# One row of score, state and y matmuls per chunk, keys transposed from the rotated rows, and an engine order set by a list of moves

## The chip, the cores and the metric

The kernel runs on one core of a Trainium2 chip. A core has five engines that run side by side, each with its own in-order instruction stream: TensorE (PE) multiplies matrices and writes to PSUM, a small memory of eight banks of 2 KB per partition; VectorE (DVE), ScalarE (ACT) and GpSimd (POOL) work on tensors elementwise; SyncE (SP) only issues transfers (DMAs). Engines wait for each other through semaphores. The metric is device time of one execution in microseconds. The kernel before took 684.2 us (median of three runs, 683.13 to 686.0).

## The reference

A gated linear recurrence (GateLoop) on 4 x 8 heads, 768 steps, head size 48, is followed by a SwiGLU feed-forward on 3072 tokens (384 to 1536 to 384). All is fp32. What is computed:

```python
mag = np.sqrt(a_re * a_re + a_im * a_im)
scale = np.minimum(mag, 0.999) / (mag + 1e-06)
a_re_n, a_im_n = (a_re * scale, a_im * scale)
for t in range(S):
    new_re = ar * S_re - ai * S_im
    new_im = ar * S_im + ai * S_re
    kv = np.einsum('bhd,bhe->bhde', k[:, :, t], v[:, :, t])
    S_re, S_im = (new_re + kv, new_im)
    y[:, :, t] = np.einsum('bhd,bhde->bhe', q[:, :, t], S_re)
...
rms = np.sqrt(np.mean(x * x, axis=-1, keepdims=True) + 1e-06)
xn = x / rms * rms_g
g = xn @ w_gate
silu = g * (1.0 / (1.0 + np.exp(-g)))
val = xn @ w_val
return (silu * val @ w_out).astype(np.float32)
```

## The kernel before

**Chunks.** The 768 steps of each of the 4 sequences are cut into 6 chunks of 128, which gives 24 chunks (n = 0 to 23). Within a chunk the recurrence is a masked attention; between chunks a state per head is carried on. The gates are turned into sizes and angles beforehand, and keys and queries are scaled and rotated by them (`gates`, lines 1138 to 1234). The rotation leaves six row blocks of 128 partitions x 256 columns per chunk (three times the cosine, three times the sine part; columns 0 to 127 are keys, 128 to 255 queries), in `rot` and, from chunk 4 on, also in `kin`. Six DMAs on SP (line 1229) put these rows into `kq`, 96 partitions x 8 heads x 256. Units of two chunks share the gate work; chunks 0 and 1 are units of their own.

**One chunk on TensorE** (`attend`, lines 1247 to 1355):

- *Scores* S, in two halves a = 0, 1 of four heads each: 16 fp32 matmuls of 32 output rows each (line 1262), then one COPY_PREDICATED on DVE per half ("the mask") that takes the causal part into `am`. For chunks 0 to 3 the halves use banks 4 and 5; from chunk 4 (`LATER`) on both use bank 5, so the second half waits for the first half's mask.
- *y* into bank 6: 16 matmuls on `am` and `ve` and, unless the sequence starts, 16 on the old state and the queries.
- *Transposes*: eight of 96 x 128 keys out of `kq`, copied by ACT to `kt`; *state* T: 24 matmuls of `kt` and `vn` into bank 5, then two DVE operations that make the new state. The last chunk of a sequence (n = 5, 11, 17, 23) has neither.
- *norm*: square of y, its sum over features by a matmul with ones (bank 7), then `ssv` on ACT, then a power of -1/2 on POOL (line 1335), a broadcast of that number, and a product on DVE that writes `xT`, the input of the feed-forward, out of bank 6.

Scores, y and state are written in column tiles of 32 (the profile shows them as 96*32 and 128*32); all other matmuls use the array whole (128*128 or 96*128).

**Feed-forward.** Pairs of chunks make 12 groups. Groups 0 and 1 use plain products; from group 2 on gate and value products follow a fast scheme with 15 products on sums of blocks (`joint`, `STEPS`, `PRODUCTS`), and the output product uses seven block products (`down`).

**Order.** Nothing is issued as it is written. `fast` fills a list of operations with estimated durations and dependencies (`Flow.add`, line 579); a whole PSUM bank counts as one place. `Flow.schedule` (line 617) plays that list through: at each step the engine that is free first takes its ready operation with the earliest due time. Due times follow from the last user backwards, plus a table of shifts by stage (`flow.shift`). The result is a fixed order for each engine. In the first 62 us of the plan, `Flow.warm` puts idle matmuls ("fillers", on `rot`, bank 3) where the plan has TensorE wait (lines 707 to 713). Their number comes from the planned gap: one for each 0.43 us at first, one for each 0.26 us later.

**Weights** arrive as pairs of 32-bit words and are converted by ACT and DVE (`narrow`); POOL issues these transfers in the order of pieces.

Of the kernel before, what the change touches and what calls it, by code (L numbers as in the profile page):

```python
# [14 lines left out]
ALU = mybir.AluOpType  # L15
# [485 lines left out]
class Flow:  # L501
# [15 lines left out]
    def __init__(self, nc, rooms):  # L517
        self.nc = nc
        self.rooms = rooms
        self.ops = []  # L520
        self.seen = {}
        self.stage = None
        self.shift = {}
        self.warm = None
        self.fillers = []

# [52 lines left out]
    def add(self, eng, calls, dur, reads=(), writes=(), table=None, land=None, due=None, after=(), behind=(), late=None, mode=None, group=None):  # L579
        over = self.OVERLAP.get(eng, 0.0) if land is None else 0.0  # L580
        shy = eng == "POOL" and land is None and calls[0][0] == self.nc.gpsimd.tensor_tensor
# [12 lines left out]

    def dates(self):
        users = [[] for _ in self.ops]
        self.next = [[] for _ in self.ops]
        for op in self.ops:
# [18 lines left out]
    def schedule(self):  # L617
        users = self.dates()
        left = [len(op["deps"]) + len(op["behind"]) for op in self.ops]
# [4 lines left out]
        mode = last = None  # L624
# [21 lines left out]
        while True:  # L646
            best = None
            for eng, ops in waiting.items():
                if ops:
# [29 lines left out]
            for o in waiting[eng]:  # L679
                if ready[o["i"]] > t + 1e-9:  # L680
# [9 lines left out]
            if eng in self.patient:  # L690
# [13 lines left out]
            if eng == "PE":  # L704
                dur += self.between(o, last)
                mode, last = o["mode"], o
            if eng == "PE" and self.warm and not claimed and t < self.warm["until"] and all("end" in x for x in self.warm["after"]):
                since = max([free["PE"]] + [x["end"] + 0.06 for x in self.warm["after"]])
                step = 0.26 if recent else 0.43
                n = int((t - since - 0.25) / step)  # L710
                if n > 0:
                    self.fillers.append((order - 0.5, n))
                    recent.append((since, since + step * n))
# [35 lines left out]
def fast(tc, ctx, qT, kT, v, a_re, a_im, w_gate, w_val, w_out, rms_g, out, H, bad):  # L749
# [171 lines left out]
    room("pad0", [P, 3])  # L921
# [47 lines left out]
    for t in banks[4:6]:  # L969
# [42 lines left out]
    def fetch(i, piece, raw, eng):  # L1012
# [12 lines left out]
        pace = dict(load=1.9 + 1.0e-3 * raw.shape[1], lead=1.2) if eng == "POOL" else dict(slow=2.5)  # L1025
# [48 lines left out]
    SUMMED = ()  # L1074
    LIGHT = (0, 1, 2)
    SENT = range(4, N - 2)
    turn = {}
    moved = {}
    HOLD = 1
# [58 lines left out]
    def gates(u):  # L1138
# [72 lines left out]
        for i, n_ in enumerate(ns):  # L1211
# [11 lines left out]
            rows[n_] = [o[:, j] for o in turned for j in range(ND)]  # L1223
        for i, n_ in enumerate(ns):
# [4 lines left out]
            moved[n_] = [dma(kq[r:D2:2 * ND], x, "SP", slow=0.3) for r, x in enumerate(rows[n_])]  # L1229
# [17 lines left out]
    def attend(n):  # L1247
# [12 lines left out]
        k, q = kq[:, :, 0:C], kq[:, :, C:2 * C]  # L1260
        for a in range(2):
# [11 lines left out]
            o = am[:, a * HH:(a + 1) * HH]  # L1273
            add("DVE", [(nc.vector.copy_predicated, (), dict(out=pairs(o), mask=mask, data=pairs(s)))],
                0.2 + 1.04e-3 * HH * C, [causal, s, o], [o])
        flow.stage = "y", n
# [476 lines left out]
```

## Time and profile before

| | |
|---|---|
| median of three runs | 684.2 us (683.13 to 686.0) |
| the profiled execution | 682.97 us |
| its span, first to last instruction | 681.2 us |
| busy: TensorE, VectorE, ScalarE, GpSimd | 646.5, 556.8, 499.4, 66.8 us |
| mean granted TensorE clock | 0.999 |

The page of the profile gives totals, the waits name who waited for whom, the windows give busy time by stretch, and the timeline lists instructions in order of time. A timeline row has the start, the time from first start to last end, the engine, the line, the operation with out<-in, the stationary and moving shapes, and xN, the number of records; fp32 products have two records each, transposes one. A square bracket gives idle time of that engine before the row and who ended it. Nearly all instructions carry line 746, since one loop issues them all, so groups are told apart by names: `bank<-kq` is S, `bank<-am,ve` and `bank<-kq,state` together are y, `bank<-vn,kt` is T, `bank<-ident,kq` the transposes. A row's second number overlaps the next row; for the cost on TensorE the distance from start to start counts.

### The profile page before, as it was taken

The numbers are of one execution on the slowest core, as the hardware profiler recorded it, in microseconds if no ns is written. First come the engines' busy times: TensorE is split into PE (matmuls) and PEld (weight loads), VectorE is DVE, ScalarE is ACT, GpSimd is POOL, SyncE is SP. The second block draws the span as 40 slices with busy tenths as digits, with TensorE's granted clock in tenths as the row PEclk, the third lists the DMA queues.
The fourth block names the chain that finished last, engine by engine and source line by source line (L and its number), as shares of the span: only waits on it lengthen the run. The fifth ranks groups of instructions, "written<-read, shape, count | busy, mean of one in ns | idle before, by whom it ended". The sixth has DMA issues, their size and how long they took to land.

```text
span 681.2 us, 19019 instructions
## 1 busy us (share of the span) xinstructions
PE 646.5 (95%) x7914; PEld 603.4 (89%) x7917; DVE 556.8 (82%) x1026; ACT 499.4 (73%) x864; POOL 66.8 (10%) x109
## 2 busy tenths in 40 slices
PE   0689999999999999999999999999999999999997
PEld 0678877886899999999999999998999999999997
DVE  8989999989998969879989869789879787246463
ACT  8649657995685774775778777777669686699872
POOL 3121034011000100011010100101000000000000
PEclk9999999999999999999999999999999999999999
DMA  9798483454425521354543522455250437725410
GB/s 280 264 240 238 125 239 98 113 125 94 106 51 99 140 36 52 95 114 86 142 84 60 134 68 50 109 122 141 40 111 17 105 115 149 254 95 189 160 47 27
DMA packets 104155, 81.98 MB, mean 120 GB/s; under 512 B 41952, under 2 KB 94560, under 8 KB 104064
## 3 DMA queue, kind: packets, MB, share of 16 engines
q1 hardware_dynamic: 98560, 64.68, 35.5%
q0 software_dynamic: 4416, 15.35, 10.9%
q8 instruction: 63, 1.03, 0.6%
q10 hardware_dynamic: 1088, 0.69, 0.3%
q14 instruction: 28, 0.23, 0.1%
HBM read 55.84 MB, written 4.72 MB: 89 GB/s over the span
## 4 chain that ended last, share of the span: by engine, by line
issue 33%; PE 32%; DVE 13%; DMA 9%; ACT 7%; POOL 2%; SPq 2%; POOLq 0%; DVEq 0%; ACTq 0%
PE bank L746 32%; DMA sq<-rs 4%; SPq L746 2%; ACT L746 2%; DMA wo<-in_w_gate_dram 2%; DVE hT L746 2%; DVE turns L746 2%; ACT t L746 1%; DVE wo L746 1%; POOL rs L746 1%; DVE rot L746 1%; DVE t L746 1%; ACT in L746 1%; DVE wv L746 1%; DVE wg L746 1%
## 5 line engine op out<-in xcount | busy, mean ns | idle before, releaser
L746 PE MATMUL bank<-wo,hT 128*128 128x192 f32 (+1 forms) x696 | 140.8, 350 | 0.0
L746 PEld LDWEIGHTS bank<-wo,hT 128*128 128x128 f32 x696 | 115.0, 190 | 11.6 <-DVE hT L746 0.5
L746 PE MATMUL bank<-xT,wg 128*128 128x128 f32 (+1 forms) x488 | 84.3, 305 | 1.6 <-ACT sg L746 1.6
L746 PE MATMUL bank<-xT,wv 128*128 128x128 f32 (+1 forms) x488 | 82.6, 301 | 0.0
L746 ACT ACT_TABLE_LOAD x57 | 73.1, 1283 | 9.7 <-DVE rot L746 4.8
L746 PEld LDWEIGHTS bank<-xT,wg 128*128 128x128 f32 x488 | 70.6, 191 | 6.8 <-ACT sg L746 1.8
L746 ACT ACTIVATE hT<-bank 128x512 f32<-128x512 f32 x100 | 58.1, 594 | 21.5 <-PE bank L746 19.2
L746 PEld LDWEIGHTS bank<-xT,wv 128*128 128x128 f32 x488 | 70.0, 192 | 3.2 <-issue 0.2
L746 POOL TENSOR_TENSOR rs<-ssv,mhalf 128x1 f32<-128x1 f32 x24 | 21.0, 877 | 442.0 <-ACT ssv L746 388.7
L746 DVE TENSOR_TENSOR hT<-hT 128x768 f32<-128x768 f32 (+1 forms) x60 | 51.7, 863 | 0.4
L746 PE MATMUL bank<-yg,wg 128*128 128x128 f32 x320 | 50.7, 281 | 0.0
L746 PE MATMUL bank<-yg,wv 128*128 128x128 f32 x320 | 48.8, 275 | 0.0
L746 ACT ACTIVATE bank<-bank 128x512 f32<-128x512 f32 x60 | 35.1, 586 | 18.2 <-PE bank L746 11.6
L746 DVE TENSOR_TENSOR hT<-bank,hT 128x512 f32<-128x512 f32 x50 | 34.4, 688 | 13.5 <-ACT bank L746 5.4
L746 DVE COPY_PREDICATED am<-causal,bank 128x512 f32<-128x512 int32 x48 | 34.8, 734 | 12.7 <-PE bank L746 12.5
L746 ACT ACTIVATE sg<-bank 128x256 f32<-128x256 f32 (+1 forms) x72 | 38.4, 534 | 8.7 <-DVE bank L746 4.7
L746 PE MATMUL bank<-sums,hT 128*128 128x192 f32 x240 | 44.7, 329 | 0.0
L746 PEld LDWEIGHTS bank<-yg,wg 128*128 128x128 f32 x320 | 42.2, 191 | 1.3 <-issue 0.2
L746 PEld LDWEIGHTS bank<-yg,wv 128*128 128x128 f32 x320 | 42.2, 192 | 0.0
L746 PEld LDWEIGHTS bank<-sums,hT 128*128 128x128 f32 x240 | 39.1, 190 | 0.3
L746 ACT ACTIVATE turns<-in 128x768 f32<-128x768 f32 (+1 forms) x39 | 30.6, 792 | 11.2 <-DVE in L746 5.8
L746 PEld LDWEIGHTS bank<-kq 96*32 96x32 f32 x1536 | 30.4, 110 | 9.4 <-issue 3.6
(217 smaller groups left out, 1451.4 us busy)
## 6 DMA issues: line engine op xcount, KB each, us to landing
kq<-rot SPq DMA_DIRECT2D x84, 128.0 KB, 2.4
kq<-kin SPq DMA_DIRECT2D x60, 128.0 KB, 2.6
kin<-in_q_dram SPq DMA_DIRECT2D x24, 192.0 KB, 3.0
kin<-in_k_dram SPq DMA_DIRECT2D x24, 192.0 KB, 3.7
in<-in_a_re_dram SPq DMA_DIRECT2D x11, 384.0 KB, 4.2
in<-in_a_im_dram SPq DMA_DIRECT2D x11, 384.0 KB, 4.5
out_dram<-ot SPq DMA_DIRECT2D x22, 192.0 KB, 2.2
vn<-in_v_dram SPq DMA_DIRECT2D x20, 192.0 KB, 2.9
```

What stands on the lines that cost most here:

```text
L746: fn(*args, **kw)
```

## The change

1. *Row.* S of both halves, T and y (in two parts) of one chunk are bound into a chain from chunk 4 on: the planner, once it has placed one link, places the next link as TensorE's next operation. T goes ahead of y.
2. *Banks.* From chunk 4 on the halves of the scores use banks 5 and 6 (6 is also y's), state uses bank 7, the transposes banks 7 and 5. Bank 6 is cleared once at the start, as 4 and 5 were.
3. *Transposes* read the six rotated row blocks (128 x 128 each) in place of `kq`, three in each half; ACT puts the columns in order as it copies.
4. *Two roots.* For chunks 0 and 1 the power on POOL becomes a reciprocal root and a square on ACT and two operations on DVE.
5. *Planner.* Fillers are counted in another way, modelled durations of some transfers change, the table of shifts is another, masks and transposes have stages of their own, and after a first pass a list of some 1,200 moves (`flow.moves`: put operation o behind operation x) rearranges the order of all five engines; a second pass only computes times for that order, with fillers counted anew. In the second pass a chain need not stay unbroken: its links keep their order, and a move can put another operation between two of them.

```diff
@@ class Flow
+    def chain(self, ops):
+        for o in ops[1:]:
+            ops[0]["deps"] |= {d for d in o["deps"] if d < ops[0]["i"]}
+        for o, x in zip(ops, ops[1:]):
+            o["then"] = x["i"]
+            x["deps"].add(o["i"])
...
     def schedule(self):
+        self.run()
+        if self.moves:
...
+            for eng, moves in self.moves.items():
+                out = {o for o, _ in moves}
+                line = [o for o in lines[eng] if o not in out]
+                for o, behind in moves:
+                    line.insert(line.index(behind) + 1 if behind >= 0 else 0, o)
+                lines[eng] = line
+            self.fillers = []
+            self.run(lines)
...
+                if eng == "PE" and bound is not None and not lines:
+                    ops = [o for o in ops if o["i"] == bound]
...
-                step = 0.26 if recent else 0.43
-                n = int((t - since - 0.25) / step)
+                left_ = t - since - 0.25
+                hot = sum(e - max(b, since - 4.0) for b, e in recent if e > since - 4.0)
+                n = int(left_ / 0.24 if hot >= 2.0 else left_ / 0.43 if left_ < 3.9 else 9 + (left_ - 3.9) / 0.24)
@@ fast
-    for t in banks[4:6]:
+    for t in banks[4:7]:
         fill(t, 0.0, eng="DVE", due=-300.0)
...
-        pace = dict(load=1.9 + 1.0e-3 * raw.shape[1], lead=1.2) if eng == "POOL" else dict(slow=2.5)
+        pace = dict(load=1.9 + (0.8e-3 if i < 4 else 1.0e-3) * raw.shape[1], lead=1.2) if eng == "POOL" else dict(slow=2.5)
...
+            k_rows[n_] = [x[:, 0:C] for x in rows[n_]]
...
-            moved[n_] = [dma(kq[r:D2:2 * ND], x, "SP", slow=0.3) for r, x in enumerate(rows[n_])]
+            moved[n_] = [dma(kq[r:D2:2 * ND], x, "SP", slow=0.3 if n_ < 2 else 0.8) for r, x in enumerate(rows[n_])]
@@ attend
+        if not last:
+            kt = kts[0]
+            flow.stage = "kt", n
+            for a in range(2):
+                ps = banks[7 - 3 * a] if n < LATER else banks[7 - 2 * a]
+                kp = ps[:, 0:ND * P].rearrange("t (j x) -> t j x", j=ND)
+                ks = k_rows[n][a * ND:(a + 1) * ND]
+                calls = [(nc.tensor.transpose, (kp[:, j], ks[j], ident), {}) for j in range(ND)]
+                add("PE", calls, ND * 0.115, [*ks, ident], [kp])
+                o = kt.rearrange("t h (l a j) -> t a h l j", a=2, j=ND)[:, a]
+                act(o, kp.rearrange("t j (l h) -> t h l j", h=H), AF.Copy)
+        chain = []
         for a in range(2):
-            ps = banks[4 + a] if n < LATER else banks[5]
+            ps = banks[4 + a] if n < LATER else banks[5 + a]
...
-            mms(list_, HH // 2 * 0.285, due=EARLY.get(n), mode=BLK)
+            chain.append(mms(list_, HH // 2 * 0.285, due=EARLY.get(n), mode=BLK))
...
+        if not last:
+            ps = banks[5 if n < LATER else 7][0:D2, 0:DM]
+            chain.append(mms([(st[c * BLK:(c + 1) * BLK, h], kt[:, h, c * BLK:(c + 1) * BLK], vv[:, h], True, True)
+                 for h in range(H) for c in range(3)], H * 0.1, mode=BLK))
...
-        order = [lines[c][i] for i in range(len(lines[0])) for c in range(4)]
-        mms(order, len(order) * mm_time(C) / 4, mode=BLK)
+        early = 1 if first else 2
+        for part in (range(early), range(early, len(lines[0]))):
+            chain.append(mms([lines[c][i] for i in part for c in range(4)], len(part) * mm_time(C), mode=BLK))
+        if n >= LATER:
+            flow.chain(chain)
...
+        if n in NEWTON:
+            x, y = rss[n % 2], news[n % 2]
+            act(x, sv, AF.Abs_reciprocal_sqrt)
+            act(y, x, AF.Square)
+            stt(y, y, -0.5, sv, ALU.mult)
+            stt(x, y, 1.5, x, ALU.add)
+        else:
+            add("POOL", [(nc.gpsimd.tensor_tensor, (), dict(out=rss[n % 2], in0=sv, in1=mhalf,
+                                                            op=ALU.pow))], 0.56, [sv, mhalf], [rss[n % 2]])
...
+    flow.moves = {
+        "POOL": (
+            (9, 0), (2, 9), (11, 12), (15, 11), (4, 13), (17, 148), (5, 17), (10, 5), (14, 143),
...
```

More of the change, by code (lines that the diff above doesn't have):

```diff
@@ L525, in __init__ @@
         self.fillers = []
+        self.moves = {}
     def delay(self, o, x):
@@ L597, in dates @@
         self.next = [[] for _ in self.ops]
+        for op in self.ops:
+            op.pop("landed", None)
+            op.pop("end", None)
         for op in self.ops:
@@ L617, in schedule, with run @@
     def schedule(self):
+        self.run()
+        if self.moves:
+            lines = {}
+            for o in sorted(self.ops, key=lambda o: o["order"]):
+                lines.setdefault(o["eng"], []).append(o["i"])
+            for eng, moves in self.moves.items():
[6 more added lines that the diff above has]
+            self.run(lines)
+    def run(self, lines=None):
         users = self.dates()
+        turn = dict.fromkeys(lines or (), 0)
         left = [len(op["deps"]) + len(op["behind"]) for op in self.ops]
@@ L623, in schedule @@
         table = None
-        mode = last = None
+        mode = last = bound = None
         for op in self.ops:
@@ L679, in schedule @@
             for o in waiting[eng]:
-                if ready[o["i"]] > t + 1e-9:
+                if ready[o["i"]] > t + 1e-9 or eng == "PE" and bound is not None and not lines and o["i"] != bound or lines and o["i"] != lines[eng][turn[eng]]:
                     continue
@@ L689, in schedule @@
             o = pick[1]
-            if eng in self.patient:
+            if lines:
+                turn[eng] += 1
+            elif eng in self.patient:
                 for x in waiting[eng]:
@@ L920, in fast @@
     most = room("most", [P, 1])
-    room("pad0", [P, 3])
+    news = [room(f"new{i}", [P, 1]) for i in range(2)]
+    room("pad0", [P, 1])
     W = 4 * P
@@ new lines, in fast @@
+        ("look", 10): -15.7, ("look", 12): -0.1, ("look", 17): -50.1, ("mask", 3): -62.9, ("mask", 6): -3.4,
+        ("mask", 11): -48.4, ("mask", 16): -30.8, ("mask", 22): -57.2, ("mask", 23): -53.7, ("norm", 7): 0.3,
+        ("norm", 8): -3.5, ("norm", 9): -1.0, ("norm", 10): -13.9, ("norm", 17): 11.2, ("norm", 20): -4.5,
+        ("norm", 22): 0.1, ("norm", 23): -33.7, ("raw", 0): -8.9, ("root", 7): -5.6, ("root", 10): 71.9,
+        ("root", 11): 44.5, ("root", 12): 25.9, ("rot", 0): -3.5, ("rot", 5): 19.5, ("rot", 6): 75.5,
@@ new lines, in fast @@
+        ("rot", 7): 25.0, ("rot", 9): 5.0, ("rot", 10): 22.7, ("rot", 11): 0.1, ("rot", 12): -1.8,
+        ("scale", 0): -8.7, ("size", 0): -2.3, ("size", 2): -1.9, ("size", 3): 1.2, ("size", 4): -67.2,
+        ("size", 5): 22.7, ("size", 6): 16.1, ("size", 8): 40.2, ("size", 9): 0.3, ("size", 10): 28.1,
+        ("size", 11): 49.7, ("size", 12): 5.9, ("state", 2): 39.4, ("turn", 0): 2.2, ("turn", 1): -9.0,
+        ("turn", 3): 36.6, ("turn", 4): -5.8, ("turn", 7): -0.2, ("turn", 9): 52.9, ("turn", 10): -2.5,
@@ new lines, in fast @@
+        ("turn", 11): 1.8, ("turn", 12): 0.1, ("w", 1): 75.8, ("w", 2): -0.6, ("w", 3): -4.1, ("w", 6): 27.7,
+        ("w", 9): -3.1, ("w", 10): 66.5, ("y", 0): 6.0, ("y", 2): -1.5, ("y", 6): 0.2,
+    }
+    flow.moves = {
+        "POOL": (
+            (9, 0), (2, 9), (11, 12), (15, 11), (4, 13), (17, 148), (5, 17), (10, 5), (14, 143),
+            (6, 126), (7, 6), (149, 154), (179, 184), (197, 2326),
+        ),
+        "ACT": (
[42 rows of a table added]
+        ),
+        "DVE": (
[66 rows of a table added]
+        ),
[33 rows of a table added]
+        ),
[32 rows of a table added]
+        ),
```

79 lines of the change are left out of this document (32 added, 47 removed), and 173 rows, old and new, of the table filler.

## The prediction, made before the changed kernel was run

> **What bounds the kernel now.** I read the page first, then TensorE's waits, then two windows.
>
> ```profile
> span 681.2 us, 19019 instructions
> ...
> PE 646.5 (95%) x7914; PEld 603.4 (89%) x7917; DVE 556.8 (82%) x1026; ACT 499.4 (73%) x864; POOL 66.8 (10%) x109
> ```
> ```profile
> PE bank L746 <- DVE ot L746: 16.9, 1, 16.9
> PE bank L746 <- DVE rot L746: 6.4, 1, 6.4
> PE bank L746 <- ACT sg L746: 1.6, 1, 1.6
> ```
> ```profile
> 0.00:52.00 52.00, 26.31 (x450) 24.52 (x451) 45.03 (x76) 34.27 (x60) 14.10 (x37) 1.00 0.88 263
> 120.00:620.00 500.00, 497.42 (x6360) 468.48 (x6365) 416.16 (x792) 375.26 (x647) 35.35 (x55) 1.00 0.43 100
> ```
>
> The first window column after the length is TensorE's busy time. From 120 to 620 us TensorE is busy for 497.4 of 500 us, at full clock: this stretch gets shorter only if TensorE has less to do. Nearly all its idle time (16.9 + 6.4 us) is in the first 26 us. So there are two places: what TensorE spends in the stretch, and when the stretch begins.
>
> **Part 1, what a row saves.** Busy time hides one thing: what a change between whole-array matmuls and 32-column tiles costs. It shows in distances from start to start.
>
> ```profile
> 513.14 0.61 PE L746 MATMUL bank<-yg,wv 128*128 128x128 f32 x4
> 513.68 0.77 PE L746 MATMUL bank<-kq 96*32 96x128 f32 x32
> 514.38 0.71 PE L746 MATMUL bank<-ve,in 128*128 128x128 f32 x4
> 514.93 0.61 PE L746 MATMUL bank<-ve,kq 128*128 128x128 f32 x4
> 515.37 0.61 PE L746 MATMUL bank<-xT,wg 128*128 128x128 f32 x4
> ```
> ```profile
> 35.19 1.33 PE L746 MATMUL bank<-kq 96*32 96x128 f32 x64
> 36.46 0.94 PE L746 MATMUL bank<-ident,kq 96*128 96x96 f32 x8
> 37.33 1.08 PE L746 MATMUL bank<-am,ve 128*32 128x128 f32 x32
> ```
> ```profile
> 555.36 0.43 PE L746 MATMUL bank<-am,ve 128*32 128x128 f32 x8
> ...
> 557.15 0.86 PE L746 MATMUL bank<-vn,kt 128*32 128x48 f32 x48
> 557.94 0.71 PE L746 MATMUL bank<-ve,rot 128*128 128x128 f32 x4
> ```
>
> A block of four plain records takes 515.37 - 514.93 = 0.44. The block ahead of the scores takes 513.68 - 513.14 = 0.54 (+0.10), the block behind them 0.55 (+0.11). The half alone takes 514.38 - 513.68 = 0.70, but two halves in a row 36.46 - 35.19 = 1.27, so the second adds 0.57 and 0.13 of the 0.70 is the way out. One excursion into tiles costs 0.10 + 0.13 + 0.11, some 0.33 us. In the last fence y takes 557.15 - 555.36 = 1.79 when T follows at once; T then takes 0.79 with its way out, 0.66 without.
>
> I counted excursions on TensorE from chunk 4 on; these are the first and the last of 64:
>
> ```profile
> 123.32 0.77 PE L746 MATMUL bank<-kq 96*32 96x128 f32 x32
> ...
> 619.28 0.43 PE L746 MATMUL bank<-am,ve 128*32 128x128 f32 x8
> ```
>
> That is 3.2 for each of 20 chunks (most often S, S, then y with T). With one row each there are 20. Gross: 44 x 0.33 = **-14.5 us**.
>
> **Part 2, what the row waits for.** In a row, y stands right behind S and T, and needs both masks. That the early part of y reads only the first half does not help from chunk 4 on: y writes bank 6, which now holds the second half's scores until its mask has read them.
>
> ```profile
> 36.05 1.36 DVE L746 COPY_PREDICATED am<-causal,bank 128x512 f32<-128x512 int32 x2 [1.42 <-PE bank L746]
> ```
>
> Here DVE stood idle for the scores. First scores at 35.19, first mask at 36.05 (0.86 later), y at 37.33, so y can start 2.14 us after the first scores (the two records end at 37.41). TensorE reaches y after 2 x 0.57 + 0.66 = 1.80 with T, and after 1.14 without it. It stands for 0.34 us in 16 chunks and for 1.0 us in the four that end a sequence: 5.4 + 4.0 = 9.4 us. Behind the waiting y everything on TensorE queues: the feed-forward products, and so ACT's and DVE's evictions. Where a block of products is moved ahead of y, the stall is covered for the price of one more excursion, 0.33. That pays only for the four: 5.4 + 4 x 0.33 = **+6.7 us**. I take that, since the moves can do it.
>
> Next, a mask that is late. DVE is busy for 416 of these 500 us, and its operation in front must end first.
>
> ```profile
> 126.05 0.73 DVE L746 COPY_PREDICATED am<-causal,bank 128x512 f32<-128x512 int32 x1
> ...
> 618.28 0.74 DVE L746 COPY_PREDICATED am<-causal,bank 128x512 f32<-128x512 int32 x1
> ```
> ```profile
> 616.51 0.77 PE L746 MATMUL bank<-kq 96*32 96x128 f32 x32
> ```
>
> These are the first and last of 40 masks; the distance from scores to mask is 2.73 for the first (scores at 123.32) and 1.77 for the last. Their median is 1.04, so 0.18 above the least, 0.86; the mean without the two longest (10.2 and 5.6) is 1.20, so 0.34 above. Nothing on TensorE waited for most of these, so the order had no reason to make them prompt. Bounds: 0 to 0.95 us (a 768-column product in front) for each chunk, 0 to 19 us in all. I take 0.15 for each, near the median: **+3.0 us**.
>
> Other waits of the row cost little. T needs `kt`, but the transposes no longer wait for the DMAs into `kq`. Scores of chunk n+1 now need bank 6, that is `xT` of chunk n.
>
> ```profile
> 318.00 0.56 DVE L746 TENSOR_TENSOR xT<-bank,row 128x384 f32<-128x384 f32 x1
> ```
> ```profile
> 320.09 0.77 PE L746 MATMUL bank<-kq 96*32 96x128 f32 x32
> ```
>
> Here (chunks 11 and 12) the scores stood behind it anyway. Where they did not, they move back by a few us into the feed-forward's products; price 0 to 1 us each for some five chunks, I take 0. The next load of `kin` (SP) and the next rotation (DVE) now also wait for the second chunk's transposes, behind which SP's value loads and moves queue; they waited for the six moves before. I take 0, upper bound 2 us.
>
> **Part 3, transposes.**
>
> ```profile
> 207.79 0.50 PE L746 MATMUL bank<-ident,kq 96*128 96x96 f32 x4
> 208.13 1.17 PE L746 MATMUL bank<-wo,hT 128*128 128x192 f32 x6
> ```
>
> Four took 208.13 - 207.79 = 0.34. Three of 128 columns at 0.44 / 4 = 0.11 give 0.33. Over 40 halves that is **0** (-1 to +1). ACT's copies keep their 384 elements.
>
> **Part 4, the start.**
>
> ```profile
> 25.67 4.64 PE L746 MATMUL bank<-rot 128*128 128x128 f32 x20 [6.36 <-DVE rot L746]
> 29.67 5.59 PE L746 MATMUL bank<-rot 128*128 128x128 f32 x42
> ...
> 51.36 2.84 PE L746 MATMUL bank<-xT,wg 128*128 128x128 f32 x24
> ...
> 63.81 2.86 PE L746 MATMUL bank<-xT,wg 128*128 128x256 f32 x12 [1.57 <-ACT sg L746]
> ```
> ```profile
> 31.58 0.49 POOL L746 COPY seen<-kq 96x1 f32<-96x1 f32 x1 [2.92 <-DMA kq<-rot]
> ...
> 40.30 2.20 POOL L746 TENSOR_TENSOR rs<-ssv,mhalf 128x1 f32<-128x1 f32 x1 [8.23 <-ACT ssv L746]
> ...
> 42.58 0.80 POOL L746 DMA_DIRECT2D wo<-in_w_gate_dram  x1
> ```
> ```profile
> 55.41 1.68 ACT L746 ACTIVATE wo<-wo 128x1536 int32<-128x1536 uint32 x1 [1.50 <-DMA wo<-in_w_gate_dram]
> ...
> 59.71 1.28 ACT L746 ACT_TABLE_LOAD   x1
> 61.00 0.84 ACT L746 ACTIVATE in<-in 128x768 f32<-128x768 f32 x1
> ```
>
> POOL's power takes 2.2 us and holds the weight transfer behind it. That landed at 55.41, ACT's conversion of it stood in front of the first silu, and TensorE lost 1.57 us at 63.81. With the roots on ACT and DVE the transfer can go 2 us earlier: **-1.6 us**. The root itself gains nothing in chunk 0: a table load of 1.28 and four small operations also end some 2.2 us later. In the row above, ACT goes on 1.29 us after a load begins. (The Trainium skill, "ScalarE: Activation LUTs", section "What ACT_TABLE_LOAD costs", states a drain of some 1.38 us on top of 1.28; by it the first root would come 1.4 us later than here and the sum would be 677.4. The row above shows no such drain.)
>
> The fillers are 62 records, 31 matmuls, and the scores start at 35.19, though POOL saw `kq` landed at 31.58: 3.6 us late, since the plan expected a later landing. A tighter plan could win these 3.6; but chunk 1 and the weights' conversion stand behind, so I take **-1.4**. The other bound: 31 fillers at 0.43 are a planned gap of some 13.5 us, for which the new count gives 9 + 9.6 / 0.24 = 49, that is 18 more at 5.59 / 21 = 0.27, **+4.8 us**. The clearing of bank 6 lies under DVE's wait for its first input.
>
> **Sum** against the profiled execution, 682.97 us: -14.5 + 6.7 + 3.0 + 0 - 1.6 - 1.4 = -7.8, so 675.2. It lies 1.2 us under the median of the runs, so I forecast **676 us**.
>
> **The rivals.**
>
> *The row runs without waits* (660 to 671). Masks come on time, products fill every gap, the start wins its 3.6: -14.5 + 6.7 - 5.2 = -13, or 671 on the median's scale, and less where the moves also shorten the rest of the start. For it: 11 of the 40 masks found DVE idle. Against it: DVE is over 80% busy.
>
> *The wait takes back what the switches cost* (681 to 687.6). The four short chunks keep their 4.0 and masks are late by 0.34 as before: -14.5 + 9.4 + 6.8 = +1.7, less 3.0 at the start gives 683. That the moves break the rows up again, so that the change does not do what it says, ends here too.
>
> *Slower: late masks.* Place: y in each row, with all of TensorE behind it. Without the start's 3.0, and with 9.4 of least stall, the row loses from 5.1 / 20 = 0.26 us of lateness on; with them from 0.41. At 0.7, less than one 768-column product in front, it is -14.5 + 9.4 + 14 - 3 = +5.9, so 690 us.
>
> **How the numbers follow.** About 0.5% (3.4 us) is what a measurement of this kernel can tell from no change. Forecast (671 to 681) 0.48, without waits 0.18, taken back 0.19, slower 0.15. Faster, below 680.8: 0.66; the same, 0.19; slower 0.15. To leave no more than 0.2 out, the range takes in most of the second case and all of the third: 664 to 688.
>
> **What would show it.** Right: on TensorE's timeline `kq` x64, then `vn,kt`, then `am,ve`, 20 excursions and some more from chunk 4 on; TensorE's waits gain a line for DVE `am` of 6 to 10 us, a third of a us each; `rs` on POOL gone in the first 50 us; the product at 63.81 without its wait. Wrong: waits for `am` above 15 us, rows broken up into over 40 excursions, or scores that start after 37 us behind more than 62 filler records. The forecast fails low if the first product of the feed-forward starts well before 48 us.

## The result, and the profile after

The changed kernel takes 690.12 us (median of 20 runs, 684.38 to 694.54), the kernel before on the same chip 685.77 us (20 runs, 681.73 to 692.79). The ratio is 1.0053, with a 95% interval of 1.003 to 1.0076: the change makes the kernel some 3.6 us slower, where 8 us less were forecast. All ratios leave out runs that are more than 1.5% above the fastest run of their kernel, in experiments 4 and 6 two of twelve and in experiment 8 four. The profiled execution of the changed kernel takes 686.97 us with a span of 685.2, that of the kernel before 682.97 with 681.2, so the two profiles differ by about as much as the medians (+4.0), and can be set against each other stage by stage.

The head of the page after, and what TensorE waited for (in all, how often, longest):

```profile
span 685.2 us, 18981 instructions
...
PE 641.6 (94%) x7883; PEld 600.4 (88%) x7883; DVE 559.0 (82%) x1031; ACT 490.7 (72%) x859; POOL 62.2 (9%) x107
```
```profile
PE bank L781 <- DVE rot L781: 26.9, 3, 25.7
PE bank L781 <- DVE am L781: 5.2, 11, 1.4
PE bank L781 <- DMA decay<-ends: 2.0, 1, 2.0
PE bank L781 <- DVE xT L781: 1.6, 3, 1.1
```

TensorE is busy for 4.9 us less than before, and the span is 4.0 longer: the work shrank, and about nine microseconds of new idle time came in. Some 3.3 of the nine lie ahead of 28 us (26.6 us of waits there, 23.3 before, since fewer idle matmuls fill the time); the scores of chunk 0 start at 33.63 all the same, 1.6 us earlier than before. Of the other lines the prediction had `am`, and `xT` at nothing; `decay`, 2.0 us in one piece, it did not have.

To see where, I cut both spans where the scores of chunk 4 start, the first chunk of the new row, and where TensorE ends. First the kernel before, then the changed one, in windows (start and end, length, then the busy time of TensorE, its weight loads, VectorE, ScalarE and GpSimd, the granted clock, the DMA share and GB/s):

```profile
34.00:123.32 89.32, 84.76 (x1056) 70.98 (x1055) 83.19 (x107) 60.15 (x91) 21.19 (x21) 1.00 0.68 189
123.32:677.00 553.68, 551.14 (x6798) 522.03 (x6801) 443.54 (x860) 413.74 (x733) 35.90 (x56) 1.00 0.42 100
```
```profile
34.00:125.49 91.49, 86.70 (x1065) 72.41 (x1054) 86.31 (x117) 69.74 (x104) 18.64 (x21) 1.00 0.66 185
125.49:680.20 554.71, 547.56 (x6776) 521.20 (x6775) 442.94 (x856) 396.37 (x717) 35.72 (x57) 1.00 0.42 100
```

At the cut the changed kernel has issued one block of feed-forward products less (2.60 us in the kernel before) and two groups of transposes more (0.66). At equal work its scores of chunk 4 would stand at 125.49 + 2.60 - 0.66 = 127.43, **4.1 us behind**; I had forecast 3.0 ahead. The rows take 554.71 - 2.60 + 0.66 = 552.77 against 553.68, **0.9 us less**; I had forecast 4.8 less. The last 0.8 us come after TensorE's end. 4.1 - 0.9 + 0.8 = 4.0.

**The rows.** TensorE's timeline of the changed kernel at chunk 9, a row in one piece (start, duration, operation, number of records; in brackets the idle time before it and what ended it):

```profile
252.83 1.33 PE L781 MATMUL bank<-kq 96*32 96x128 f32 x64
253.97 0.86 PE L781 MATMUL bank<-vn,kt 128*32 128x48 f32 x48
255.09 0.49 PE L781 MATMUL bank<-am,ve 128*32 128x128 f32 x7 [0.27 <-DVE am L781]
...
257.09 0.71 PE L781 MATMUL bank<-xT,wg 128*128 128x128 f32 x4
```

The row stands as foreseen: both halves of the scores, then T, then y, with a wait for the mask. It takes 257.09 - 252.83 = 4.26. But only 8 of the 20 rows are like this. In 11 others, moves in the order have put products, a norm or transposes between the scores and y (most often between T and y; the last chunk of a sequence has no T), and in chunk 4 one filler stands there. That is two excursions into tiles, in the last chunk three; I count 33 excursions where there were 64. TensorE's waits from chunk 4 on, in the changed kernel, are 6.6 us; in the kernel before the same view adds up to 2.1:

```profile
PE bank L781 <- DVE am L781: 3.8, 10, 0.9
PE bank L781 <- DVE xT L781: 1.3, 2, 1.1
PE bank L781 <- DVE hT L781: 0.8, 2, 0.4
PE bank L781 <- ACT bank L781: 0.7, 3, 0.3
```

**The start.** VectorE's and TensorE's timeline of the changed kernel between 40 and 50 us, where the kernel before had `xT` of chunk 0 done and was on its way to its first product at 51.36:

```profile
40.56 1.75 DVE L781 SCALAR_TENSOR_TENSOR wg<-hT,wg 128x1536 int32<-128x1536 int32 x1
...
44.02 0.55 DVE L781 TENSOR_TENSOR xT<-yg,bank 128x384 f32<-128x384 f32 x1
44.48 1.75 DVE L781 TENSOR_TENSOR turns<-in,turns 128x1536 f32<-128x1536 f32 x1
44.62 0.55 PE L781 MATMUL bank<-ident,rot 128*128 128x128 f32 x3 [0.30 <-DVE xT L781]
45.10 0.77 PE L781 MATMUL bank<-kq 96*32 96x128 f32 x32
46.15 0.95 DVE L781 TENSOR_TENSOR t<-t,t 128x768 f32<-128x768 f32 x1
46.26 0.77 PE L781 MATMUL bank<-kq 96*32 96x128 f32 x32
47.02 1.33 DVE L781 COPY_PREDICATED am<-causal,bank 128x512 f32<-128x512 int32 x2
```

The scores of chunk 1 stand behind `xT` of chunk 0, and their masks behind size work of chunk 2 (`turns`, `t`); y of chunk 1 and all that follows from it come later, and the first product starts at 54.22, 2.9 us behind. Then TensorE loses more at two places, again from its timeline:

```profile
83.86 1.33 PE L781 MATMUL bank<-kq 96*32 96x128 f32 x64 [2.04 <-DMA decay<-ends]
85.12 2.86 PE L781 MATMUL bank<-xT,wg 128*128 128x256 f32 x12
...
103.01 0.43 PE L781 MATMUL bank<-am,ve 128*32 128x128 f32 x8 [1.43 <-DVE am L781]
```

The scores of chunk 2 wait 2.04 us, y of chunk 3 waits 1.43. (In between, the block at 64.94 no longer has the wait of 1.57 that it had before, so 1.6 us come back there.) The wait named `decay` has several semaphores behind it; SP's queue shows what was last, the six moves of chunk 2 into `kq`, issued on both sides of three loads of values:

```profile
70.04 0.58 SPq L781 DMA_DIRECT2D kq<-rot  x1
70.66 1.94 SPq L781 DMA_DIRECT2D ve<-in_v_dram  x3
72.70 1.68 SPq L781 DMA_DIRECT2D kq<-rot  x2
...
76.99 1.84 SPq L781 DMA_DIRECT2D kq<-rot  x3
```

### The profile page after: what moved, and what is told of

It reads as the page before. It is cut to its first block, busy times and chain, and to the rows that moved or that the text cites. A ratio compares the mean times of both kernels' runs of the same rounds, so it can differ in the third digit from the quotient of the medians.

```text
span 685.2 us, 18981 instructions
## 1 busy us (share of the span) xinstructions
PE 641.6 (94%) x7883; PEld 600.4 (88%) x7883; DVE 559.0 (82%) x1031; ACT 490.7 (72%) x859; POOL 62.2 (9%) x107
## 3 DMA queue, kind: packets, MB, share of 16 engines
q8 instruction: 63, 1.03, 0.6%
## 4 chain that ended last, share of the span: by engine, by line
PE 54%; issue 18%; DVE 13%; DMA 8%; ACT 5%; SPq 1%; POOL 1%; DVEq 0%; POOLq 0%; ACTq 0%
PE bank L781 54%; DMA sq<-rs 3%; DVE am L781 2%; DVE turns L781 2%; DVE hT L781 2%; DMA decay<-ends 2%; DVE wg L781 1%; SPq L781 1%; DMA wo<-in_w_gate_dram 1%; DVE t L781 1%; DVE rot L781 1%; ACT L781 1%; ACT bank L781 1%; ACT hT L781 1%; DMA row<-sq 1%
## 5 line engine op out<-in xcount | busy, mean ns | idle before, releaser
L781 POOL TENSOR_TENSOR rs<-ssv,mhalf 128x1 f32<-128x1 f32 x22 | 17.1, 777 | 446.5 <-ACT ssv L781 402.9
L781 DVE TENSOR_TENSOR hT<-hT 128x768 f32<-128x768 f32 (+1 forms) x60 | 51.5, 863 | 0.8
L781 PE MATMUL bank<-am,ve 128*32 128x128 f32 x768 | 40.2, 275 | 5.1 <-DVE am L781 4.9
L781 ACT ACTIVATE sg<-bank 128x512 f32<-128x512 f32 (+1 forms) x72 | 38.2, 534 | 8.9 <-PE bank L781 5.0
L781 DVE TENSOR_TENSOR bank<-bank,hT 128x512 f32<-128x512 f32 x30 | 20.9, 697 | 22.8 <-ACT hT L781 19.7
```

Of the source, the lines that this page charges most:

```text
L781: fn(*args, **kw)
```

## The experiments

The order of the changed kernel comes from a planner and its list of moves (1,530 of them), and any edit would make it plan anew. So each experiment takes the changed kernel's final order as a fixed list for each engine, and edits that. In the diffs an operation is named by its number, and `(350, 348)` puts operation 350 right behind 348 on that engine. The last experiment is the list with no edit. Ratios are to the kernel before, on the same chip; the changed kernel's 1.0053 was measured beside other runs of it, so a difference between that ratio and one below (0.001 is 0.7 us) carries both intervals. For stages I use the profiled execution of each kernel: "scores of chunk 4" is their start there (125.49 in the changed kernel), "the stretch" is from there to TensorE's end (554.7).

**1. The two roots on GpSimd again**

```diff
-    NEWTON = (0, 1)
+    NEWTON = ()
```

> The roots of chunks 0 and 1 go back to GpSimd's power; every engine keeps the order of the changed kernel. Theory A (the new way of the root costs the start: ScalarE, then two steps on VectorE that stand behind operations of 1.75 us): from ssv(0) to xT(0) it takes about 3 us as before (40.21 to 43.22) and not 5.5 (38.55 to 44.02), the first feed-forward product comes at about 52 us and not 54.2, and the time falls by 1.5 to 2.5 us. Theory B (the order of the start costs it: the scores of chunk 1 stand behind xT(0) on TensorE, its masks behind work of chunk 2 on VectorE): the first product moves by less than 1 us and the time by less than 0.7 us.

Measured: ratio 1.0076 (1.0043 to 1.011). GpSimd's timeline of this kernel:

```profile
39.08 1.29 POOL L781 COPY seen<-kq 96x1 f32<-96x1 f32 x1 [7.04 <-DMA kq<-rot]
40.52 2.37 POOL L781 TENSOR_TENSOR rs<-ssv,mhalf 128x1 f32<-128x1 f32 x1
```

The power takes 2.37 us, behind a copy that waits for a landing, and yet `xT` of chunk 0 starts at 44.27, against 44.02 with the new root. The new root cost nothing in chunk 0; the start was not lost there. For the time as a whole this is no clean test, and the ratio is not told apart from the changed kernel's: the first product starts at 56.29, 2.1 us later than in the changed kernel and not within 1 us of it as theory B had it, with 22 filler records in front, and the scores of chunk 2 wait 4.21 us.

**2. The start in the order of before**

The operations planned for the first 65 us go back to the order of the kernel before, with the roots on GpSimd; the keys of chunk 1 are transposed into two other banks, which that order needs.

```diff
-    NEWTON = (0, 1)
+    NEWTON = ()
...
-                ps = banks[7 - 3 * a] if n < LATER else banks[7 - 2 * a]
+                ps = banks[2 * a] if n == 1 else banks[7 - 3 * a] if n < LATER else banks[7 - 2 * a]
```

> Of the changed kernel, the first 65 us (planned) are put into the order that every engine had before, with the roots on GpSimd; the keys of chunk 1 are transposed into banks 0 and 2, so that its scores need not wait for xT(0). From there on everything is in the order of the changed kernel. Theory B (order of the start): the masks of chunk 1 come at about 41 us and not 47, the first product at about 51.5 us and not 54.2, and the time falls by 2 to 3.5 us. Theory A (only the root): as in the run with the roots alone. Theory C (VectorE is full from 34 to 84 us, so that whatever comes earlier is waited for later): first product at 51.5, but by 90 us nothing is left of it and the time is the same within 0.7 us.

Measured: ratio 0.9995 (0.9972 to 1.0018), so (1.0053 - 0.9995) x 685.8 = 4.0 us less than the changed kernel; the two intervals do not meet. VectorE's timeline:

```profile
40.56 1.33 DVE L781 COPY_PREDICATED am<-causal,bank 128x512 f32<-128x512 int32 x2
41.78 0.54 DVE L781 TENSOR_TENSOR xT<-yg,bank 128x384 f32<-128x384 f32 x1
```

The masks of chunk 1 now stand ahead of `xT` of chunk 0, 6.5 us earlier than in the changed kernel; the scores of chunk 2 start at 83.09 without a wait, those of chunk 4 at 124.91, and the stretch is 553.6. By the ratio, the order of the first 65 us is what the changed kernel loses at the start. The profile doesn't show where: the first product starts at 53.35 (expected: 51.5, changed kernel: 54.22), and the scores of chunk 4 only 0.6 us earlier than in the changed kernel's profile, which is what theory C said of the trace. One candidate is the wait ahead of the scores of chunk 2, which differs from execution to execution with the changed kernel's start (see why the prediction was wrong).

**3. The moves of chunk 2 first**

The six moves of chunk 2 go in one piece ahead of the loads of values on SP, and the masks of chunk 3 one scan ahead on VectorE.

```diff
-    later = {}
+    later = {'SP': [(350, 348), (347, 350), (351, 347), (349, 351), (352, 349)], 'DVE': [(406, 532), (404, 406), (537, 404)]}
```

> In the changed kernel the six moves of chunk 2's rotated rows go ahead of the loads of v and of chunk 3 on SyncE's queue, and the two masks of chunk 3 one scan ahead on VectorE. Theory D (two waits in the chunks written separately, 2.04 us ahead of the scores of chunk 2 and 1.43 us ahead of y(3), are a good part of what is lost by 120 us, and the 2.04 us, which the trace puts down to a decay transfer, is the late landing of chunk 2's keys): the scores of chunk 2 start at about 81.8 us without a wait, the wait of y(3) falls to about 0.8 us, the time falls by 2 to 2.7 us. Rival (VectorE's work for chunks 2 and 3 is what is late): the waits move on to later operations of these chunks, the time falls by less than 0.7 us.

Measured: ratio 1.0012 (0.998 to 1.0043), 2.8 us less than the changed kernel by these ratios, though the two intervals overlap. SP's queue and TensorE's timeline of this kernel:

```profile
70.68 4.97 SPq L781 DMA_DIRECT2D kq<-rot  x6
```
```profile
82.38 1.33 PE L781 MATMUL bank<-kq 96*32 96x128 f32 x64
...
101.54 0.42 PE L781 MATMUL bank<-am,ve 128*32 128x128 f32 x8 [1.05 <-DVE am L781]
```

The scores of chunk 2 wait no more, so the wait put down to `decay` was for these moves. The masks of chunk 3 gained only 0.4 of the 1.43. The scores of chunk 4 start at 124.11, 1.4 earlier.

**4. The rows without masks**

From chunk 4 on y reads a constant tile in place of `am`, and the second mask reads the other bank, so that y has nothing to wait for. It leaves the masked scores out of y.

```diff
             o = am[:, a * HH:(a + 1) * HH]
+            if n >= LATER:
+                s = banks[5].rearrange("s (h t) -> s h t", h=HH)
...
-                todo.append((vf[:, m, g * BLK:(g + 1) * BLK], am[:, h]))
+                todo.append((vf[:, m, g * BLK:(g + 1) * BLK], am[:, h] if n < LATER else causal[:, 0]))
```

> From chunk 4 on y takes a constant table in place of the masked scores, and the second mask reads the bank of the first scores, so that neither a mask nor its bank holds y back; the order is that of the changed kernel. The output leaves out the masked scores of these chunks. Theory E (the waits of y for its masks took the saving of the rows back): the 3.5 us of waits for the masks from chunk 4 on are gone and the time falls by 3 to 4 us. Rival F (a row saves little even without its wait, and TensorE is held by what VectorE and ScalarE deliver): other waits (for xT, hT, copied keys) take their place and the time falls by less than 1.5 us.

Measured: ratio 1.0001 (0.9968 to 1.0034), 3.6 us less than the changed kernel; the stretch is 550.19, 4.5 less. The row of chunk 9 takes 3.69 us where it took 4.26, so the wait cost 0.57 though only 0.27 of it shows as idle. From the start of T to the start of y 1.12 us pass in the changed kernel (253.97 to 255.09), and 0.63 here; from there to the next block 2.00 and 1.92. So it is nearly all lost ahead of y, where the records of T still run out and count as busy, and y itself is hardly slower. The start of this kernel is by no means the same, though nothing there was edited. Three windows in its profile, with the same columns as above:

```profile
84.00:88.00 4.00, 0.75 (x25) 0.79 (x29) 1.79 (x2) 2.78 (x4) 0.90 (x2) 0.79 0.97 204
88.00:92.00 4.00, 4.00 (x56) 3.44 (x47) 2.99 (x5) 0.74 (x1) 0.00 (x0) 0.50 0.66 202
92.00:96.00 4.00, 4.00 (x101) 3.35 (x103) 3.87 (x5) 0.60 (x1) 0.43 (x1) 0.86 0.02 4
```

The scores of chunk 2 waited 4.3 us, with the DMA engines 97% busy, and then TensorE ran for some 6 us at about half its clock: the second window has 56 records where the third has 101. Chunk 4 came 7.7 us late in this execution, more than the rows gained in it.

**5 and 6. Start and chunk 2 together, and the new roots in the old start**

Experiment 5 joins experiments 2 and 3, and moves two operations on ScalarE; experiment 6 is experiment 2 with the roots on ScalarE and VectorE, right behind the first state (`NEWTON = (0, 1)` stays, and no move is made).

```diff
-    later = {}
+    later = {'SP': [(344, 342), (341, 344), (345, 341), (343, 345), (346, 343)], 'DVE': [(400, 526), (398, 400), (531, 398)], 'ACT': [(238, 236), (301, 251)]}
```

> Both edits that shortened the start together: the first 65 us in the order of before with the roots on GpSimd (as in the run with the start's order back), the keys of chunk 1 copied one place earlier on ScalarE, the moves of chunk 2 first on SyncE's queue and the masks of chunk 3 one scan ahead. Theory B+D (two separate losses, 4.0 and 2.8 us by the ratios of their runs): they add up to some 5 to 6.5 us, a ratio to before of 0.993 to 0.996, and no run with a long wait ahead of the scores of chunk 2 is left, so the spread is small. Theory C (both are one loss, VectorE's work up to 100 us): no better than the better of the two, 0.998 to 1.001.

> As the run with the start's order back, but the two roots stay on ScalarE with their two steps on VectorE, placed right behind state(0) and ahead of the masks of chunk 1. Against that run only the roots differ. Theory A' (the new root is slower by its table load of 1.28 us and its place on VectorE): xT(0) one to two us later, y(1) not held, the first product 0 to 1 us later, the time 0 to 1.5 us longer. Theory A'' (the new root is as fast once it stands well, and GpSimd's transfers of weights start earlier): the same within 0.7 us or up to 1.5 us faster.

Measured: 1.0012 (0.9989 to 1.0035) and 1.0039 (1.0005 to 1.0072). The two gains did not add up. TensorE's timeline of experiment 5 has one reason, and its first product is 2.9 us later than in experiment 2:

```profile
51.58 1.50 PE L781 MATMUL bank<-vn,kt 128*32 128x48 f32 x48 [3.12 <-DMA vn<-in_v_dram]
```

T of chunk 1 waited for its values, issued at 42.03 and landed some 9 us later (from 42 to 52 us the DMA engines move 309 GB/s here, and weights are under way); in experiment 2 it waited 0.92, in experiment 6 4.12. So experiment 6 doesn't price the root in the order of before: its first product is late (55.99) by that landing, while `xT` of chunk 0 starts at 41.94 against 41.78. That much agrees with experiment 1. The rest stays open. Here, too, the early part shows little behind it: in experiments 2, 5 and 6 the first product starts at 53.35, 56.28 and 55.99, and the scores of chunk 4 at 124.91, 127.49 and 127.68; experiment 10 has its first product at 49.03 and these scores at 127.33.

**7. All rows broken**

In each of the 8 unbroken rows a block of products is put ahead of y, as the order does in the other 12.

```diff
-    later = {}
+    later = {'PE': [(449, 817), (935, 1097), (1139, 1310), (1373, 1549), (1582, 1580), (1418, 1582), (1871, 2042), (2128, 2314), (2205, 2527), (2561, 2559), (2374, 2561), (2418, 2774)]}
```

> In the changed kernel the eight rows that run without a break (chunks 6, 9, 10, 12, 16, 19, 20, 22) get one block of products between their parts, so that the mask is ready behind it. Theory G (by the trace an unbroken row takes 4.26 us with its wait, a row broken once 4.04 with its further edge): the eight waits of some 0.3 us go, one excursion each comes back, and the time falls by up to 1.8 us; from chunk 4 to the end of TensorE the trace shortens by 1 to 2 us. Theory H (the prediction's 0.33 us for an excursion): eight excursions cost 2.6 us and the waits give 2.6 back: no change.

Measured: ratio 1.0139 (1.0097 to 1.0182, 6 runs), the slowest of all; the stretch is 560.7. Breaking a row is free only where nothing waits for the block that is moved. VectorE's and TensorE's timelines of this kernel at chunk 16:

```profile
447.64 0.69 DVE L781 TENSOR_TENSOR hT<-bank,hT 128x512 f32<-128x512 f32 x1 [2.04 <-PE bank L781]
448.25 1.32 DVE L781 COPY_PREDICATED am<-causal,bank 128x512 f32<-128x512 int32 x2
```
```profile
449.62 0.49 PE L781 MATMUL bank<-am,ve 128*32 128x128 f32 x7 [2.09 <-DVE am L781]
```

An eviction of the feed-forward (`hT`) stands ahead of the masks on VectorE. It waited for products that the moved block had delayed, the masks waited behind it, and y behind them. Chunk 20 has a like wait of 1.89 us, there behind a sum of the output (`ot`). So my expectation was wrong, and it is no test of the price of a whole row.

**8. Whole rows without masks**

Experiment 4, with the blocks moved out of broken rows.

```diff
-    later = {}
+    later = {'PE': [(637, 293), (811, 607), (673, 669), (882, 881), (1171, 1187), (1418, 1421), (1467, 1466), (1662, 1660), (1656, 1662), (1960, 1955), (2374, 2370), (2785, 2598)]}
```

> As the run of the rows without masks, and in addition the blocks of products that break twelve rows are put ahead of the row, so that all twenty chunks from chunk 4 on run in one row. The output leaves out the masked scores of these chunks. Against that run, by the prediction's price of 0.33 us for an excursion (thirteen excursions fewer): 4 us less. By the rows of the changed profile (only the two edges of products, about 0.2 us): 2 to 2.6 us less. Rival (products that come earlier or later than planned wait for their operands): no gain, with new waits for hT and for banks.

Measured: ratio 0.9985 (0.9946 to 1.0023), not told apart from experiment 4's 1.0001; 23 excursions in place of 32. TensorE's busy time in the stretch falls by 0.9 us (543.76 from 544.63), but the stretch is 0.9 longer (551.10 from 550.19). Ten of the 13 whole rows with T and all of y take 3.68 to 3.69 (the others 3.92 to 4.32), and yet new waits stand elsewhere: 1.7 us for ACT `hT`, 1.5 for `sg`, 1.5 for DVE `hT`, 0.9 for `sq` (experiment 4 has 0.8 each for `sg` and DVE `hT` and none for the others). Most are waits for what ScalarE and VectorE make of products, so I read them as the price of products that come at another time; no run shows this block by block.

**9. The two banks of the scores swapped**

The first half of the scores goes into bank 6 and the second into bank 5, with the edits of experiment 3; in chunk 18 the two masks also change places on VectorE. y writes bank 6, which is now free once the *first* mask has read it. Nothing is left out.

```diff
-            ps = banks[4 + a] if n < LATER else banks[5 + a]
+            ps = banks[4 + a] if n < LATER else banks[6 - a]
...
-    later = {}
+    later = {'SP': [(350, 348), (347, 350), (351, 347), (349, 351), (352, 349)], 'DVE': [(406, 532), (404, 406), (537, 404), (2280, 2278)]}
```

> The run with chunk 2's moves first, and from chunk 4 on the two halves of the scores exchange their banks: the first half goes to bank 6, which y takes next, the second to bank 5. So the first part of y waits for the first mask alone, and the second mask runs beside it. Theory E (the masks' waits take the saving of the rows): of the 3.8 us that y waits for masks from chunk 4 on less than 1 us is left, the stretch from the scores of chunk 4 to the end of TensorE falls from 554.7 to about 550.5 us, the ratio to before from 1.0012 to about 0.996. Rival (the scores now wait earlier for xT of the chunk before, which reads bank 6: 1.3 us in two chunks so far, 0.7 us more each; or VectorE's order moves the waits on): the stretch falls by less than 1.5 us.

Measured: 683.89 us (12 runs, 679.81 to 688.53), ratio **0.9943 (0.9916 to 0.997)**: faster than both kernels. The waits for masks from chunk 4 on are one of 0.25 us, where they were 3.8 in all. TensorE's waits and timeline:

```profile
PE bank L781 <- DVE xT L781: 2.5, 3, 1.4
PE bank L781 <- issue: 1.6, 2, 1.1
PE bank L781 <- DVE am L781: 1.2, 2, 0.9
```
```profile
250.95 1.33 PE L781 MATMUL bank<-kq 96*32 96x128 f32 x64
252.09 0.81 PE L781 MATMUL bank<-vn,kt 128*32 128x48 f32 x45
252.72 0.30 PE L781 MATMUL bank<-am,ve 128*32 128x128 f32 x1
...
254.67 0.60 PE L781 MATMUL bank<-xT,wg 128*128 128x128 f32 x3
...
303.78 1.33 PE L781 MATMUL bank<-kq 96*32 96x128 f32 x64 [1.37 <-DVE xT L781]
```

The row of chunk 9 takes 254.67 - 250.95 = 3.72, as without masks. The first half of the scores now needs the bank of `xT`, so some scores wait for that (1.37 here), and two rows stand for "issue", 0.42 and 1.15 us, which names no cause; experiment 4 has the same two, 0.55 and 1.03. In the profiled execution the stretch is 553.72, only 1.0 less than in the changed kernel, which is what the rival said: against the changed kernel 3.5 us of mask waits are gone, and 0.9 more for `xT`, 0.9 for `ends` and 1.6 of "issue" have come. The ratios say more, 4.7 us between experiments 3 and 9 and 4.5 between 2 and 10 (the latter's stretch is 2.9 shorter), each from two chips. How much of the gain is the banks' own is therefore known only roughly.

**10. Swapped banks with the old start**

Experiments 2 and 9 together, the values of chunk 1 loaded earlier, and at most two filler matmuls in later groups.

```diff
-    later = {}
+    later = {'SP': [(234, 296)], 'DVE': [(400, 526), (398, 400), (531, 398), (2274, 2272)]}
```

> The run with the start's order back, with the banks of the scores exchanged as well, the rows of v for state(1) loaded ahead of chunk 2's, at most two filler products ahead of the last broadcasts of the start, and the masks of chunk 3 one scan ahead. Theory: state(1) no longer waits for its rows of v (0.9 us there, up to 4.1 in like kernels), the first product comes at 50 to 51 us and not 53.4, the rows gain 4 us as in the run with the exchange alone, and the ratio to before is 0.992 to 0.995. Theory C (VectorE is what the first 100 us wait for): the first product comes earlier, but by the scores of chunk 4 the run stands where the start's order back alone stood (124.9 us), and only the rows' gain is left, 0.995 to 0.997.

Measured: 682.88 us (12 runs, 681.23 to 685.02), ratio 0.9929 (0.9904 to 0.9954), not told apart from experiment 9. TensorE's timeline and a window:

```profile
49.03 2.84 PE L781 MATMUL bank<-xT,wg 128*128 128x128 f32 x24
...
62.88 3.53 PE L781 MATMUL bank<-xT,wg 128*128 128x256 f32 x8 [2.96 <-ACT sg L781]
```
```profile
62.88:66.88 4.00, 4.00 (x11) 3.24 (x12) 3.74 (x5) 4.00 (x5) 0.18 (x1) 0.57 1.03 297
```

The first product came at 49.03, 5.2 us ahead of the changed kernel. Then the products waited 2.96 us for the first silu, as the kernel before does with 1.57, and went on at 0.57 of the clock; the scores of chunk 4 start at 127.33, *later* than the 125.49 of the changed kernel. An early start by itself gave nothing in the profiled execution (685.02 us). The stretch is 550.7, 4.0 us less.

**11. The changed kernel's list, unedited**

> The changed kernel once more, on the chip and beside the runs of before that the others use. If its start differs from execution to execution (kernels with the very same start showed the scores of chunk 2 at 83.9, 85.4, 87.3 and 87.4 us), its median lies 2 to 4 us above its best run, and its ratio to before at 1.003 to 1.008; if the first profile was the rule, at 1.005 with little spread.

Measured: 693.36 us (12 runs, 685.16 to 695.29), ratio 1.0068 (1.0032 to 1.0103). So the fixed list is the changed kernel, and on this chip, which also ran experiments 9 and 10, those two are 9.5 and 10.5 us below it in median. The profiled execution took 686.57 us, and its scores of chunk 2 wait 2.08 us, as in the first profile.

## Why the prediction was wrong

**Part 4, the start, failed first and by most: -3.0 foreseen, +4.1 measured, 7.1 of the 11.8 us between the sum (-7.8) and the profile (+4.0).** Its details came true. `rs` is gone from GpSimd's first 50 us, the product that waited at 63.81 waits no more (the -1.6), and the scores of chunk 0 start at 33.63, 1.6 us earlier than before (the -1.4). "The root itself gains nothing" held too: 44.27 and 44.02 for `xT` of chunk 0 with the one and the other. What failed was the step from there to the time. I took the first stage as the old one with a wait removed, and let the scores move earlier; apart from fillers, no term of the sum stood for what the new order would cost. But the change plans the whole start anew, and the new order puts the masks of chunk 1 behind size work of chunk 2, and the moves of chunk 2 around loads of values. From the scores of chunk 0 to the first product 20.59 us pass where 16.17 did. Experiments 2 and 3 price the two: 4.0 and 2.8 us by their ratios, the second hardly clear of noise, and not additive (experiment 5). That the order of the first 65 us is at fault is shown by the ratio of experiment 2; which of its moves, and on which later wait the time depends, is not. The row that speaks of it was there before: from 34.00 to 123.32 VectorE of the kernel before is busy for 83.19 of 89.32 us. My windows ended at 52 and began again at 120, so I read the fullest stretch of VectorE not at all, and "chunk 1 and the weights' conversion stand behind" served only to take less of a gain. The bound on the loss (+4.8) was drawn from fillers; that it held is an accident.

The 4.1 us are those of one execution (686.97 us, where the median is 690.12). Five executions with this same start were profiled: there the scores of chunk 2 wait 2.04, 2.08, 2.74, 4.13 and 4.33 us (the changed kernel, experiments 11, 8, 7 and 4). Behind the last three the granted clock is 0.58, 0.62 and 0.50 in the next 4 us, and the scores of chunk 4 start at 128.60, 130.23 and 133.23, where they start at 125.49 and 125.66 behind the first two. With chunk 2's moves first (experiments 3 and 9) there is no such wait, and the mean clock of an execution is 0.9985 in the median, where it is 0.9935 to 0.997 in these five kernels. By an estimate from that, 0.0015 to 0.005 of some 690 us, the clock takes 1 to 3.5 us there, in experiment 7 also behind other stops. I had no term for it.

**Part 1, the price of an excursion, was right.** In the kernel before the separate parts of a chunk take 4.60 us (two halves of the scores at 0.70, T with y 2.57, and 0.10 + 0.11 around each of the three); a row with no wait takes 3.69 + 0.21 = 3.90 (experiment 4). The difference is 0.70, where two excursions less at 0.33 make 0.66. The *count* was wrong. I let the moves break up four rows; the new order broke up twelve, and each of these, counted as a row with T and all of y, takes 4.24 (1.92 for S and T, 1.90 for y, 2 x 0.21 around them). It saves 0.36 in place of 0.70.

**Part 2, the waits.** A wait for masks of "a third of a us each" was right as far as it shows (0.27 at chunk 9). But only about half of a wait shows as idle: the one of 0.27 costs 0.57, and at that price the eight whole rows keep only 0.13 each. 12 x 0.36 + 8 x 0.13 = 5.4 us saved, where -14.5 + 6.7 + 3.0 made 4.8: near, and by compensation, since fewer rows waited and each lost more. The rest went to waits that I had priced at nothing. For bank 6 and `xT`, "I take 0": 1.3 us from chunk 4 on. Masks outside the whole rows are 1.2, `hT` and ScalarE's banks 1.5; against 2.1 of such waits in the kernel before that is 1.9 more, and 5.4 - 1.9 = 3.5 should be left. Measured are 0.9, so 2.6 us are missing. Row by row most of them can be found: against the rows without masks (experiment 4: 3.69, and 2.80 and 2.84 for chunks 12 and 6, which begin a sequence) the eight whole rows lose 5.5 us, not 8 x 0.57 = 4.6, and the rows of chunks 5, 11 and 13 are 1.1 us longer than their idle time explains. **Some 0.5 us stay unplaced.**

**Part 3** held: the two groups of transposes ahead of the cut take 0.33 us each, as foreseen.

**A slip in the sum.** The 677.4 us that the prediction gives for a longer table load are the forecast of 676 plus 1.4; the sum of 675.2 would be 676.6. Nothing else hangs on it.

**The rivals.** "Slower" gave 690 us, which is the measured median, but by luck: it named late masks as the one mechanism, and y waited for masks 5.2 us in all, below the 6 to 10 that I gave for the forecast. "The wait takes back what the switches cost" (681 to 687.6) was nearer in mechanism: its clause that the moves break the rows up again is what happened to twelve rows. But it took 3.0 us from the start, which is where it also failed. No rival had a start that loses.

Two things were argued and not shown. The row-by-row sums set single executions of two kernels against each other; the six whole rows of the changed kernel with all of y take 4.26 to 4.67, and in experiment 4 some rows take 3.85 with no wait shown. And experiment 8 shows that moving the blocks back gains nothing and brings other waits, not that no better place for them exists.

## What to carry to other kernels

When a change replaces a whole planned order, price the new order at its worst-covered stage and don't carry the old stage over with one wait removed: here the first 125 us lost more (4.1) than all the rows behind them gained (0.9). Look at which bank the *last* input frees: y waited for the second mask only because its own bank held the second half of the scores, and an exchange of two bank numbers took the mask waits from 3.8 us to 0.25 from chunk 4 on. A block of work that splits a row on the fullest engine may be what keeps the others fed; before closing the row, look at who reads its products. And take more than one profile of a kernel whose times spread: with the same start, the scores of chunk 2 waited 2.04 us in one profile and 4.33 in another.

## What was not expected of the hardware

The granted clock fell after short stops, and not after all of them. In the 4 us behind a stop of TensorE it stood at 0.50 after stops of 4.33 and 4.21 us (experiments 4 and 1), at 0.62 after 4.13 (experiment 7, chunk 2) and at 0.57 after 2.96 (experiment 10). It stood at 0.58 after 2.74 (experiment 8), at 0.57 after 2.28 (y of chunk 3 in experiment 1), and in experiment 7 after 2.09 us at 0.57, where y took 3.37 us in place of the 2.00 of the changed kernel's chunk 9:

```profile
449.60:453.00 3.40, 3.38 (x65) 2.99 (x65) 2.41 (x5) 0.00 (x0) 0.00 (x0) 0.57 0.02 5
```

Stops of 2.04 and 2.08 us ahead of the scores of chunk 2 (the changed kernel and experiment 11) had no such effect: the clock reads 1.00 in the next 4 us, and the block behind the scores takes its usual 2.86. A stop of 1.46 us (experiment 4, y of chunk 3) had one, with 0.62, and stops of 1.43 and 1.44 at the same place in the changed kernel and in experiment 2 had none. (The Trainium skill, "TensorE: Matmul & The Clock Gate", section "Part 1: The HAM clock gate (the "warmup" mystery)", states half rate after an idle window of about 3.4 us, and full rate after about as much busy time; the 4.3 us agree, the 2.09 and 2.96 us here are shorter.) So a wait of 2 to 3 us on TensorE can cost 1.4 to 1.7 us beyond what shows as idle (y at 3.37 for 2.00 after 2.09 us, a block at 4.54 for 2.86 after 2.96 us), and one cannot tell from its length alone.
